# Start and end of a six-layer cross network on TensorE: row transposes, one set of weight sums, and the last addition moved

## The chip, the cores and the metric

One Trainium2 chip, one of its cores. The metric is the time of one execution on the device in microseconds: 2319.8 us, the median of 3 runs (2318.58 to 2320.22). All times below are microseconds from the start of the profiled execution unless something else is said. PE is TensorE, DVE is VectorE, ACT is ScalarE, SP is the queue of SyncE that issues most DMAs.

## The reference

```python
B, F, D, L = 16384, 100, 16, 6
Din = min(F * D, 1024)            # 1024
# x0: (16384, 1024), ws: (6, 1024, 1024), bs: (6, 1024), all bf16
x = x0
for l in range(L):
    proj = jnp.einsum('bd,de->be', x, ws[l]) + bs[l]
    x = x0 * proj + x
return x
```

Each layer multiplies the state (16384 rows of 1024) by a weight matrix, adds a bias, multiplies by the first input and adds the old state.

## The kernel before

The rows are worked through in 16 pairs of two blocks of 512 rows, and within a pair layer by layer. The state is held transposed (features on the partitions): `xst[:, n, k, :]` is feature chunk `k` of 8 for block `n`, and `x0T` holds the pair's input in the same way. A layer is a 2x2 block product: halves of the features by the two row blocks. It is done in Strassen's manner with seven half-size products, named by a number `pid`: products 1, 2 and 4 use blocks of the weight matrix as they are, products 5, 6, 3 and 7 use sums of weight blocks, and their right-hand sides are blocks of the state or the differences T1 to T4 that DVE makes (`Ops.t`). From the second pair on, product 2 is itself split into seven quarter-size products (`inner`, L287), with the differences `ti` and the *small sums*, `pid` 8, made from block W21 of the weights.

A product's matmuls go to PSUM tiles of 128x512 (`px`). There are two pools of four banks each, `ps[0]` and `ps[1]`, which change roles from layer to layer as `psA` and `psX`. ACT evicts PSUM (`ev`, L45 and L48). DVE adds the parts (L42), multiplies by `x0T` (`f_mul`) and adds the old state (`f_add`, which writes `xst`).

All weight tiles live in one ring of 12 buffers (`wring`, tile name `wp`). `prefetch_upto` issues loads on SP ten places ahead in the fixed order 1, 2, 8, 5, 3, 6, 7, 4. In the first pair the sums do not exist yet: `emit_combo(l, pid)` makes them on DVE from the raw blocks (W12 has its own tile `w`), and `flush_saves` writes each of them to a DRAM buffer `Lc`, from which all later pairs load them. DVE is busy for 24.0 us in a first-pair layer and for 20.5 us in a later one. In the first pair's layer `l` the sums 5, 6 and 3 of layer `l+1` are made after `f_add(C1, 0, 0)`, and sum 7 of layer `l+1` and the small sums of layer `l` at the end. For the last layer of the first pair, only the small sums are left, made at the end.

After each pair but the last, SP issues a DMA transpose of the finished state into the pair's own `x0T` tile (L481) and two stores of it (L484). The x0 transposes of a following pair (L474) are issued during an earlier one. The last pair's output is treated apart: its lower feature half goes through `out_region` (L231: DMA transpose, store of 512 KB), its upper half is transposed on PE by matmuls against an identity (`out_pe`, L240), evicted by ACT and DVE, and stored in pieces of 256 KB.

The start: DMA loads of x0 rows and weights are issued from SP and ACT. The first 512 rows are loaded as rows in two halves of the features (`xrows`) and transposed on PE by `transpose_rows(h)` (L204): per feature chunk four matmuls of 128x128 against the identity, then one eviction, by ACT for even chunks and by DVE for odd ones. The second 512 rows come by one DMA transpose (L193).

The order on each engine is that of the program for ACT, DVE (`pin`) and the startup DMAs. A scheduler places the other DMAs among them, and it also inserts the waits: for data, for a ring buffer or a bank that must become free, and for one of eight DMA semaphores that are used in turn.

Of the kernel before, what the change touches and what calls it, by code (L numbers as in the profile page):

```python
# [17 lines left out]
def kernel(  # L18
# [163 lines left out]
    b_all = const.tile([P, LK], FP32, name="b_all")  # L182
    x0T_next = x0t_pool.tile([P, 2, KD, NB], BF16, name="x0T")
    xrows = [ev_pool.tile([P, KH, NB], BF16, name="ev") for _ in range(2)]
    raw = {i: wring.tile([P, KH, H], BF16, name="wp") for i in (1, 2, 4)}
    combo_st[0] = {"w12": w12_pool.tile([P, KH, H], BF16, name="w12")}
    for h in range(2):
        pin(nc.sync.dma_start(xrows[h][:], x0[0:NB, h * H:(h + 1) * H].rearrange("(r p) d -> p r d", p=P)))  # L188
        if h == 0:
            pin(nc.scalar.dma_start(raw[1][:], w_src(0, 1)))  # L190
            pin(nc.sync.dma_start(b_rows[:], bs.rearrange("l (m p) -> (l m) p", p=P)))
    pin(nc.scalar.dma_start(raw[2][:], w_src(0, 2)))
    pin(nc.sync.dma_start_transpose(out=x0T_next[:, 1], in_=x0[NB:2 * NB, :]))  # L193
    pin(nc.scalar.dma_start(combo_st[0]["w12"][:], ws[0][0:H, H:D].rearrange("(k p) e -> p k e", p=P)))
    pin(nc.scalar.dma_start(raw[4][:], w_src(0, 4)))
    for i in raw:
# [4 lines left out]
    for _ in range(8):  # L201
        nc.tensor.matmul(warm[:], lhsT=zero[:, 0:P], rhs=zero[:], start=True, stop=True)

    def transpose_rows(h):  # L204
        for k in range(KH):
            pt = ps[1].tile([P, NB], FP32, name="px")
            for r in range(KH):
                nc.tensor.matmul(pt[:, r * P:(r + 1) * P], lhsT=xrows[h][:, r, k * P:(k + 1) * P], rhs=ident[:],
                                 start=(r == 0), stop=True, skip_group_check=True)
            dst = x0T_next[:, 0, h * KH + k, :]  # L210
            if k % 2 == 0:
                acopy(dst, pt[:])
            else:
                pin(nc.vector.tensor_copy(out=dst, in_=pt[:]))
# [10 lines left out]
    for pr in range(NPAIR):  # L225
# [11 lines left out]
            pin(nc.sync.dma_start(out[r0:r0 + NB, 0:H].rearrange("(j p) d -> p j d", p=P),  # L237
                                  xo_last["t"][:, n].rearrange("p j k r -> p j (k r)")))

        def out_pe(pts, n, ms, yo):  # L240
            for j in range(KH):
                for m in ms:
                    nc.tensor.matmul(pts[j][:, m * P:(m + 1) * P], lhsT=xst[:, n, KH + m, j * P:(j + 1) * P], rhs=ident[:],  # L243
                                     start=(m == 0), stop=True, skip_group_check=True)
                if ms[-1] != KH - 1:
                    continue
                if len(ms) == KH or j % 2 == 1:
                    acopy(yo[:, j, :], pts[j][:])
                else:
                    pin(nc.vector.tensor_copy(out=yo[:, j, :], in_=pts[j][:]))  # L250
                if j % 2 == 1:
                    r0 = pr * PR + n * NB + (j - 1) * P
                    pin(nc.sync.dma_start(out[r0:r0 + 2 * P, H:D].rearrange("(j p) d -> p j d", p=P), yo[:, j - 1:j + 1, :]))

        for l in range(L):
# [71 lines left out]
            if small:  # L327
                w2i = weights(8)
                wi = w2i[:].rearrange("p k (j e) -> p k j e", e=HE)
                b = cur.rhs(2)  # L330
                ti = cur.ti
                EA = ei_pool.tile([P, KH, NB], BF16, name="ea")
                EB = ei_pool.tile([P, KH, NB], BF16, name="eb")
                c11, c12 = (slice(0, 2), slice(0, NQ)), (slice(0, 2), slice(NQ, NB))
                c21, c22 = (slice(2, 4), slice(0, NQ)), (slice(2, 4), slice(NQ, NB))
                q2, q5, q1 = bank(), bank(), bank()
                for m in range(3):
                    mm(1, w1, pA, m, True)
                    ev(P1s, pA, m, 0)
                inner(q1, w2[:, 0:2, 0:HE], b[:, 0:2, 0:NQ], True)  # L340
                evi(EA[:, c11[0], c11[1]], q1)
                inner(q5, wi[:, 0], ti[:, 0], True)
                evi(EB[:, c22[0], c22[1]], q5)
                mm(1, w1, pA, 3, True)
                ev(P1s, pA, 3, 0)
                inner(q2, w2[:, 2:4, 0:HE], b[:, 2:4, 0:NQ], True)
                evi(EB[:, c11[0], c11[1]], q2)
                pX = [bank() for _ in range(KH)]
                w5 = weights(5)
                mm(5, w5, pX, 0, True)  # L350
                ev(P5s, pX, 0)
                inner(q1, wi[:, 1], ti[:, 1], False)
                evi(EA[:, c12[0], c12[1]], q1)
                inner(q5, wi[:, 2], b[:, 2:4, NQ:NB], False)
                evi(EB[:, c12[0], c12[1]], q5)
                mm(5, w5, pX, 1, True)
                ev(P5s, pX, 1)
                inner(q1, wi[:, 3], ti[:, 2], False)
                evi(EA[:, c22[0], c22[1]], q1)
                mm(5, w5, pX, 2, True)  # L360
                ev(P5s, pX, 2)
                inner(q1, w2[:, 2:4, HE:H], ti[:, 3], False)
                evi(EA[:, c21[0], c21[1]], q1)
                w3 = weights(3)
                mm(3, w3, pX, 0, False)
                ev(S53, pX, 0, 0)
                mm(5, w5, pX, 3, True)
                ev(P5s, pX, 3)
                for m in range(1, KH):
                    mm(3, w3, pX, m, False)  # L370
                    ev(S53, pX, m, 0)
                half_sum(EA, EA, EB, 0)
                cur.t(3)
                vtt(EA[:, c22[0], c22[1]], EA[:, c22[0], c22[1]], EB[:, c22[0], c22[1]], ADD)
                cur.t(4)
                vtt(C1[:, :, 0, :], P1s[:], EA[:], ADD)
            else:
                P2s = evt()
                for m in range(KH):
                    mm(1, w1, pA, m, True)  # L380
                    ev(P1s, pA, m, 0)
                    if step == 1 and m == 0:
                        transpose_rows(1)
                        ops.t(1)
                        for pid in (5, 6, 3):
                            emit_combo(0, pid)
                        ops.t(2)
                        emit_combo(0, 7)
                        flush_saves()
                pX2 = [bank() for _ in range(KH)]  # L390
                for m in range(KH):
                    mm(2, w2, pX2, m, True)
                    ev(P2s, pX2, m)
                pX = [bank() for _ in range(KH)]
                w5 = weights(5)
                for m in range(KH):
                    mm(5, w5, pX, m, True)
                    ev(P5s, pX, m)
                w3 = weights(3)
                for m in range(KH):  # L400
                    mm(3, w3, pX, m, False)
                    ev(S53, pX, m, 0)
                cur.t(3)
                cur.t(4)
                vtt(C1[:, :, 0, :], P1s[:], P2s[:], ADD)
            f_mul(C1, 0, 0)
            f_add(C1, 0, 0)
            if combos_next:
                for pid in (5, 6, 3):
                    emit_combo(l + 1, pid)  # L410
            w6 = weights(6)
            for m in range(KH):
                mm(6, w6, pA, m, False)
# [30 lines left out]
            else:  # L444
                n1, n0 = 1 ^ flip, flip
                pT = [bank() for _ in range(KH)]
                out_pe(pT, n1, range(KH), evt())
                c = lambda ms: C2[:, ms, 0, :]
                xs = lambda ms: xsrc[:, n0, KH:KD, :][:, ms, :]
                xz = lambda ms: x0T[:, n0, KH:KD, :][:, ms, :]  # L450
                parts = [slice(0, 2), slice(2, 3), slice(3, 4)]
                vtt(c(parts[0]), c(parts[0]), xz(parts[0]), MULT)
                vtt(c(parts[1]), c(parts[1]), xz(parts[1]), MULT)
                vtt(xs(parts[0]), c(parts[0]), xs(parts[0]), ADD)
                vtt(c(parts[2]), c(parts[2]), xz(parts[2]), MULT)
                vtt(xs(parts[1]), c(parts[1]), xs(parts[1]), ADD)
                vtt(xs(parts[2]), c(parts[2]), xs(parts[2]), ADD)
                pT2 = [psA.tile([P, NB], FP32, name="px") for _ in range(KH)]
                yo = evt()
                out_pe(pT2, n0, (0, 1, 2), yo)  # L460
                out_pe(pT2, n0, (3,), yo)
            if combos_next:
                emit_combo(l + 1, 7)
                emit_combo(l, 8)
                if l + 1 == L - 1:
                    stage_ctx.close()
                    xo_pool = ctx.enter_context(tc.tile_pool(name="xo", bufs=1))
            elif pr == 0:
                emit_combo(l, 8)
            if l == (2 if pr == 0 else 0) and not last_pair:  # L470
                x0T_next = x0t_pool.tile([P, 2, KD, NB], BF16, name="x0T")
                for n in range(2):
# [43 lines left out]
```

## Time and profile before

| what | us |
|---|---|
| median of 3 runs | 2319.8 |
| profiled execution, its time | 2319.24 |
| profiled execution, its span on the core | 2317.5 |
| PE busy (share of the span) | 2286.7 (99%) |
| DVE busy | 1992.9 (86%) |
| ACT busy | 1830.7 (79%) |
| mean granted TensorE clock | 0.999 |

The span is what the profile covers, from the first to the last instruction; 1.7 us of the execution lie around it. A busy PE is one that has matmuls in its pipeline; a matmul of 512 columns is shown as 0.38 long, but such matmuls start every 0.216, so the records overlap. Some records are missing, so a count in a line can be one or two short. In a timeline line the columns are the start, the length, the engine, the source line, the operation, what it writes and reads, its shape, how many such instructions in a row, and in brackets how long the engine had been idle and what ended that.

### The profile page before, as it was taken

Reading aid. Unit: us, or ns where it says so; the run is one execution under the profiler, and the core shown is the slowest. Engines: PE = TensorE matmul, PEld = TensorE weight load, DVE = VectorE, ACT = ScalarE, POOL = GpSimd, SP = SyncE. Lnnn points to the kernel's source line nnn. Section 1 sums busy time; section 2 is a strip of 40 time slices with the busy share of each in tenths; the row PEclk is TensorE's granted clock in tenths of the full one; section 3 lists DMA queues with packets and bytes.
Section 4 is the critical chain, followed back from the end, with each engine's and each line's share of the span. In section 5 each row is a group of like instructions: output and inputs, shape, how many; then the busy total and the mean of one; then the engine's idle time right before and its main releaser. Section 6 shows DMA issues by size and latency. Waiting matters only on the chain.

```text
span 2317.5 us, 31676 instructions
## 1 busy us (share of the span) xinstructions
PE 2286.7 (99%) x11675; PEld 1161.2 (50%) x11905; DVE 1992.9 (86%) x2232; ACT 1830.7 (79%) x2970; POOL 0.7 (0%) x6
## 2 busy tenths in 40 slices
PE   8999999999999999999999999999999999999998
PEld 3444554545555455555545454555545455554544
DVE  7997888888888888888888888888888888888888
ACT  6777887878788787878778787877878787887877
POOL 0000000000000000000000000000000000000000
PEclk9999999999999999999999999999999999999999
DMA  7759587595876959669586685966859578595763
GB/s 246 245 170 311 173 209 254 177 287 173 217 246 182 282 176 227 232 183 280 185 223 237 192 266 188 250 212 190 271 177 273 190 200 264 173 288 176 214 214 108
DMA packets 606618, 507.52 MB, mean 219 GB/s; under 512 B 391424, under 2 KB 545024, under 8 KB 606464
## 3 DMA queue, kind: packets, MB, share of 16 engines
q1 hardware_dynamic: 604352, 503.39, 72.6%
q10 hardware_dynamic: 2112, 2.10, 0.3%
q8 instruction: 94, 1.54, 0.3%
q14 instruction: 60, 0.49, 0.1%
HBM read 391.13 MB, written 49.28 MB: 190 GB/s over the span
## 4 chain that ended last, share of the span: by engine, by line
PE 92%; DVE 6%; issue 1%; DMA 1%; ACT 0%; SPq 0%; DVEq 0%
PE px L281 80%; PE px L287 12%; DVE cb L42 2%; DVE xst L42 1%; DVE wp L42 1%; DVE T L42 1%; DMA x0T<-in_x_dram 1%; DMA wp<-Lc 0%; ACT ev L45 0%; DVE ti L42 0%; SPq L188 0%; DVE ev L250 0%; DVEq L42 0%; DVEq L511 0%; PE px L243 0%
## 5 line engine op out<-in xcount | busy, mean ns | idle before, releaser
L281 PEld LDWEIGHTS <-wp 128*128 128x128 bf16 x9312 | 910.0, 98 | 1008.6 <-issue 5.8
L281 PE MATMUL px<-T,wp 128*128 128x512 bf16 x5992 | 1393.0, 379 | 9.1 <-DVE wp L42 1.3
L48 ACT ACTIVATE ev<-px,b_all 128x512 bf16<-128x512 f32 x1152 | 791.6, 687 | 223.1 <-PE px L281 215.1
L281 PE MATMUL px<-xst,wp 128*128 128x512 bf16 x2576 | 615.5, 379 | 5.5 <-DVE xst L42 2.0
L45 ACT CAST ev<-px 128x512 bf16<-128x512 f32 x798 | 466.7, 585 | 179.6 <-PE px L281 166.0
L42 DVE TENSOR_TENSOR cb<-cb,x0T 128x2048 bf16<-128x2048 bf16 (+1 forms) x386 | 469.9, 1218 | 9.9
L42 DVE TENSOR_TENSOR cb<-ev 128x1024 bf16<-128x1024 bf16 (+1 forms) x390 | 263.1, 696 | 231.8 <-ACT ev L45 231.8
L42 DVE TENSOR_TENSOR xst<-cb,xst 128x2048 bf16<-128x2048 bf16 x322 | 392.2, 1218 | 23.1 <-DVE cb L42 1.4
L48 ACT ACTIVATE cb<-px,b_all 128x512 bf16<-128x512 f32 x384 | 263.7, 687 | 67.8 <-PE px L281 55.2
L287 PEld LDWEIGHTS <-wp 128*128 128x128 bf16 x2520 | 246.5, 98 | 132.8 <-DMA wp<-Lc 5.3
L287 PE MATMUL px<-ti,wp 128*128 128x256 bf16 x1440 | 216.6, 273 | 4.9 <-DMA wp<-Lc 4.8
L45 ACT CAST ea<-px 128x512 bf16<-128x512 f32 x360 | 211.8, 588 | 0.0
L42 DVE TENSOR_TENSOR T<-xst,T 128x2048 bf16<-128x2048 bf16 x160 | 195.5, 1222 | 8.3
L42 DVE TENSOR_TENSOR T<-xst 128x2048 bf16<-128x2048 bf16 x160 | 194.9, 1218 | 0.0
L45 ACT CAST eb<-px 128x512 bf16<-128x512 f32 x270 | 160.2, 593 | 5.9 <-PE px L287 5.9
L287 PE MATMUL px<-xst,wp 128*128 128x256 bf16 x900 | 135.9, 274 | 0.0
L42 DVE TENSOR_TENSOR ea<-ea,eb 128x1024 bf16<-128x1024 bf16 (+1 forms) x180 | 99.9, 555 | 27.5 <-ACT eb L45 27.5
L281 PE MATMUL px<-x0T,wp 128*128 128x512 bf16 x514 | 122.7, 379 | 0.7
L42 DVE TENSOR_TENSOR cb<-ev,ea 128x2048 bf16<-128x2048 bf16 x90 | 109.7, 1218 | 0.0
L42 DVE TENSOR_TENSOR xst<-cb,x0T 128x2048 bf16<-128x2048 bf16 x64 | 78.4, 1225 | 2.2
L42 DVE TENSOR_TENSOR ti<-xst 128x512 bf16<-128x512 bf16 x150 | 63.2, 422 | 3.6
L42 DVE TENSOR_TENSOR ti<-xst,ti 128x512 bf16<-128x512 bf16 x150 | 62.7, 418 | 0.0
(29 smaller groups left out, 190.4 us busy)
## 6 DMA issues: line engine op xcount, KB each, us to landing
wp<-Lc SPq DMA_DIRECT2D x450, 512.0 KB, 3.8
wp<-in_ws_dram SPq DMA_DIRECT2D x285, 512.0 KB, 4.4
out_dram<-x0T SPq DMA_DIRECT2D x30, 1024.0 KB, 9.9
Lc<-wp SPq DMA_DIRECT2D x30, 512.0 KB, 3.4
w<-in_ws_dram SPq DMA_DIRECT2D x5, 512.0 KB, 5.9
wp<-in_ws_dram ACTq DMA_DIRECT2D x3, 512.0 KB, 8.0
ev<-in_x_dram SPq DMA_DIRECT2D x2, 512.0 KB, 6.7
out_dram<-xoS SPq DMA_DIRECT2D x2, 512.0 KB, 3.1
```

Source lines behind the costliest of these rows:

```text
L42: return pin(nc.vector.tensor_tensor(out=out, in0=in0, in1=in1, op=op))
L45: return pin(nc.scalar.copy(out=out, in_=in_))
L48: return pin(nc.scalar.activation(out=out, in_=in_, func=IDENT, bias=bias, scale=1.0))
L281: nc.tensor.matmul(pts[m][:], lhsT=wt[:, k, m * P:(m + 1) * P], rhs=rhs[:, k, :], start=(start and k == 0), stop=(k == KH - 1), **kw)
L287: nc.tensor.matmul(pt[:, m * NQ:(m + 1) * NQ], lhsT=w[:, k, m * P:(m + 1) * P], rhs=rhs[:, k, :], start=(start and m == 0 and k == 0), sto ...
```

## The change

Three things are changed. First, the second 512 rows of the first pair are loaded as rows, too (four loads in all, the last two into the tiles that later hold T3 and T4), and transposed on PE. The transposes of the four groups now stand before product 1, after product 1, and after product 2 (two groups); DVE's first weight sums stand between the last two groups and after them. Second, the last layer's small sums of the first pair are made after `f_add(C1, 0, 0)`, in the middle of that layer, and not at its end, and their save is issued there. Third, at the very end DVE no longer adds the old state for the last block's upper half: PE transposes the old state and the new part one after the other into the same PSUM banks, which adds them. The order of the two halves' transposes on PE is changed for that.

```diff
     xrows = [ev_pool.tile([P, KH, NB], BF16, name="ev") for _ in range(2)]
+    xrows += [t_pool.tile([P, KH, NB], BF16, name=f"T{i}") for i in (3, 4)]
...
-    for h in range(2):
-        pin(nc.sync.dma_start(xrows[h][:], x0[0:NB, h * H:(h + 1) * H].rearrange("(r p) d -> p r d", p=P)))
-        if h == 0:
-            pin(nc.scalar.dma_start(raw[1][:], w_src(0, 1)))
+    for q in range(4):
+        n, h = q // 2, q % 2
+        pin(nc.sync.dma_start(xrows[q][:], x0[n * NB:(n + 1) * NB, h * H:(h + 1) * H].rearrange("(r p) d -> p r d", p=P)))
+        if q == 0:
             pin(nc.sync.dma_start(b_rows[:], bs.rearrange("l (m p) -> (l m) p", p=P)))
+    pin(nc.scalar.dma_start(raw[1][:], w_src(0, 1)))
     pin(nc.scalar.dma_start(raw[2][:], w_src(0, 2)))
-    pin(nc.sync.dma_start_transpose(out=x0T_next[:, 1], in_=x0[NB:2 * NB, :]))
...
-    def transpose_rows(h):
+    def transpose_rows(q):
+        n, h = q // 2, q % 2
         for k in range(KH):
             pt = ps[1].tile([P, NB], FP32, name="px")
             for r in range(KH):
-                nc.tensor.matmul(pt[:, r * P:(r + 1) * P], lhsT=xrows[h][:, r, k * P:(k + 1) * P], rhs=ident[:],
+                nc.tensor.matmul(pt[:, r * P:(r + 1) * P], lhsT=xrows[q][:, r, k * P:(k + 1) * P], rhs=ident[:],
                                  start=(r == 0), stop=True, skip_group_check=True)
-            dst = x0T_next[:, 0, h * KH + k, :]
+            dst = x0T_next[:, n, h * KH + k, :]
...
-        def out_pe(pts, n, ms, yo):
+        def out_pe(pts, n, ms, src, start, yo):
             for j in range(KH):
                 for m in ms:
-                    nc.tensor.matmul(pts[j][:, m * P:(m + 1) * P], lhsT=xst[:, n, KH + m, j * P:(j + 1) * P], rhs=ident[:],
-                                     start=(m == 0), stop=True, skip_group_check=True)
-                if ms[-1] != KH - 1:
+                    nc.tensor.matmul(pts[j][:, m * P:(m + 1) * P], lhsT=src(m, j), rhs=ident[:],
+                                     start=(start and m == 0), stop=True, skip_group_check=True)
+                if yo is None:
                     continue
...
                     mm(1, w1, pA, m, True)
                     ev(P1s, pA, m, 0)
-                    if step == 1 and m == 0:
-                        transpose_rows(1)
-                        ops.t(1)
-                        for pid in (5, 6, 3):
-                            emit_combo(0, pid)
-                        ops.t(2)
-                        emit_combo(0, 7)
-                        flush_saves()
+                if step == 1:
+                    transpose_rows(1)
                 pX2 = [bank() for _ in range(KH)]
                 for m in range(KH):
                     mm(2, w2, pX2, m, True)
                     ev(P2s, pX2, m)
+                if step == 1:
+                    transpose_rows(2)
+                    ops.t(1)
+                    emit_combo(0, 5)
+                    emit_combo(0, 6)
+                    transpose_rows(3)
+                    emit_combo(0, 3)
+                    ops.t(2)
+                    emit_combo(0, 7)
+                    flush_saves()
...
             if combos_next:
                 for pid in (5, 6, 3):
                     emit_combo(l + 1, pid)
+            elif pr == 0:
+                emit_combo(l, 8)
+                flush_saves()
...
-                out_pe(pT, n1, range(KH), evt())
-                c = lambda ms: C2[:, ms, 0, :]
-                xs = lambda ms: xsrc[:, n0, KH:KD, :][:, ms, :]
-                xz = lambda ms: x0T[:, n0, KH:KD, :][:, ms, :]
-                parts = [slice(0, 2), slice(2, 3), slice(3, 4)]
-                vtt(c(parts[0]), c(parts[0]), xz(parts[0]), MULT)
-                vtt(c(parts[1]), c(parts[1]), xz(parts[1]), MULT)
-                vtt(xs(parts[0]), c(parts[0]), xs(parts[0]), ADD)
-                vtt(c(parts[2]), c(parts[2]), xz(parts[2]), MULT)
-                vtt(xs(parts[1]), c(parts[1]), xs(parts[1]), ADD)
-                vtt(xs(parts[2]), c(parts[2]), xs(parts[2]), ADD)
+                of_x = lambda n: (lambda m, j: xst[:, n, KH + m, j * P:(j + 1) * P])
+                of_c = lambda m, j: C2[:, m, 0, j * P:(j + 1) * P]
                 pT2 = [psA.tile([P, NB], FP32, name="px") for _ in range(KH)]
+                out_pe(pT2, n0, range(KH), of_x(n0), True, None)
+                out_pe(pT, n1, range(KH), of_x(n1), True, evt())
+                for ms in (slice(0, 2), slice(2, 3), slice(3, 4)):
+                    c = C2[:, ms, 0, :]
+                    vtt(c, c, x0T[:, n0, KH:KD, :][:, ms, :], MULT)
                 yo = evt()
-                out_pe(pT2, n0, (0, 1, 2), yo)
-                out_pe(pT2, n0, (3,), yo)
+                out_pe(pT2, n0, (0, 1, 2), of_c, False, None)
+                out_pe(pT2, n0, (3,), of_c, False, yo)
...
-            elif pr == 0:
-                emit_combo(l, 8)
```

In the prediction, group 0 to group 3 are the calls `transpose_rows(0)` to `transpose_rows(3)`.

## The prediction

> **What bounds the kernel now.** I read the share of the chain of waits first, then stretches of the timeline, then the waits of PE, DVE and SP inside the three stretches that the change touches.
>
> ```profile
> PE 92%; DVE 6%; issue 1%; DMA 1%; ACT 0%; SPq 0%; DVEq 0%
> ```
>
> PE carries the chain nearly everywhere. The 6% of DVE lie in the first pair, so that is where a change to DVE's order counts. The table of stretches (length, busy us and instructions of PE, weight loads, DVE, ACT and POOL, granted clock, DMA share, GB/s) sets one layer of the first pair against the second and third layer of the second pair, and against 3.4 us inside the former:
>
> ```profile
> 40.74:65.42 24.68, 24.30 (x110) 10.89 (x113) 24.04 (x26) 18.09 (x29) 0.00 (x0) 1.00 0.60 197
> 183.99:214.64 30.65, 25.66 (x123) 12.86 (x124) 20.45 (x24) 19.04 (x32) 0.00 (x0) 0.94 1.05 303
> 214.64:238.44 23.80, 23.69 (x124) 12.12 (x125) 20.53 (x24) 19.07 (x32) 0.00 (x0) 1.00 0.83 296
> 192.80:196.20 3.40, 3.32 (x15) 2.24 (x16) 0.00 (x0) 1.65 (x3) 0.00 (x0) 0.53 1.02 415
> ```
>
> A layer of the first pair lasts 24.68, four times over. Its 112 matmuls at 0.216 (12 in 2.75, each 0.38 long) need 24.2, so PE waits about half a microsecond per layer, for DVE: from 16.3 to 139 the list of waits has no other wait of DVE than the one at 16.37. The layer 183.99 to 214.64 is 6.85 longer than the next. PE's and DVE's timeline, then SP's:
>
> ```profile
> 6.88 1.19 PE L281 MATMUL px<-x0T,wp 128*128 128x512 bf16 x4
> 10.40 1.07 PE L208 MATMUL px<-ident,ev 128*128 128x128 bf16 x16 [2.32 <-DMA ev<-in_x_dram]
> 11.30 6.21 PE L281 MATMUL px<-x0T,wp 128*128 128x512 bf16 x27
> 18.79 1.47 PE L281 MATMUL px<-T,wp 128*128 128x512 bf16 x6 [1.28 <-DVE wp L42]
> 139.47 3.61 PE L281 MATMUL px<-xst,wp 128*128 128x512 bf16 x16 [0.28 <-DVE xst L42]
> 192.88 0.97 PE L287 MATMUL px<-ti,wp 128*128 128x256 bf16 x4 [4.84 <-DMA wp<-Lc]
> 16.37 1.23 DVE L42 TENSOR_TENSOR T<-x0T 128x2048 bf16<-128x2048 bf16 x1 [4.03 <-DMA x0T<-in_x_dram]
> 17.51 1.22 DVE L42 TENSOR_TENSOR wp<-w,wp 128x2048 bf16<-128x2048 bf16 x1
> 18.76 2.48 DVE L42 TENSOR_TENSOR wp<-wp 128x2048 bf16<-128x2048 bf16 x2
> 21.16 1.22 DVE L42 TENSOR_TENSOR T<-x0T,T 128x2048 bf16<-128x2048 bf16 x1
> ```
>
> ```profile
> 166.04 9.64 SPq L481 DMA_TRANSPOSE x0T<-xst  x1
> 175.73 0.57 SPq L108 DMA_DIRECT2D Lc<-wp  x1
> 177.56 5.93 SPq L484 DMA_DIRECT2D out_dram<-x0T  x2
> 183.58 7.32 SPq L94 DMA_DIRECT2D wp<-Lc  x5
> ```
>
> DVE's unbroken run starts at 16.37, with T1, when the DMA transpose of the second 512 rows lands. PE's last wait for it is at 139.47. Then SP: the weight tile of the small sums for pair 1, layer 1 is loaded at 183.58, behind the output transpose of pair 0 (which waits for DVE until 166.04), the save of the last small sums and two stores. It lands at 192.8; PE idles 4.84 and then works at a clock of 0.53 for 3.4 us. Idle and slow clock together are the 6.85. Last, DMA in 40 slices of the stretch 2311 to 2316.5:
>
> ```profile
> DMA  0089999999999999999999999999999999960000
> ```
>
> From 2311.4 to 2315.9 the DMA engines are full: the 512 KB store at 2310.36 and four of 256 KB leave without a gap.
>
> **The change part by part.** *Startup.* Removed: one DMA transpose. Added: two plain row loads, 32 transposes on PE, four evictions on ACT, four on DVE. PE's built order is now: group 0, sixteen matmuls of product 1, group 1, sixteen of product 2, groups 2 and 3, product 5. (a) Product 1's first four end as before; the fourth starts at 6.88+1.19-0.38 = 7.69, twelve follow until 10.50. The old gap (8.07 to 10.40, second rows landing) is filled. (b) Group 1 at 10.50 instead of 10.40. Product 2 needs its evictions at once: ACT first finishes product 1's fourth tile (ready 10.67, 0.69 long, the next 0.1 before its end), then the copy to 11.88. Product 2 runs 11.93 to 15.38. (c) Group 2 at 15.38. Its fourth bank is free after ACT's eviction of product 2's last tile (ready 15.55, done 16.17). Four transposes later, 0.43 from start to copy (10.40 to ACT's 10.83), DVE copies 16.67 to 17.35. T1 starts at 17.45 instead of 16.37: +1.09. (d) The sum of weight blocks 5 is then at 18.60 and 6 at 19.85. Now come DVE's two evictions of group 3, 0.61 apart (two such took 1.29, one 0.68), and weight sum 3 only at 19.85+1.14+1.22 = 22.21 against 20.02: +2.19. Product 5 begins at 19.87 (was 18.79), product 3 at 23.5 (was 22.25), so PE is ready for layer 2 at about 37.3, but DVE's xst is there at 36.87+2.19 = 39.1. DVE has no slack until 139.47, so all 2.19 arrive there; behind it PE has none either. Bounds: below, +1.1, where T1 keeps its time and only the evictions count; above, +3.5, where the new loads land 1.3 later than needed. I take 2.19, since every row in it is of the same shapes, 5 us away.
>
> What of the startup costs nothing: the SP queue is freed from 11.88 us of issuing the transpose, but its next loads are used by DVE from 29 on; they land earlier for no one. Groups 2 and 3 on PE lie before product 5, which DVE holds until 19.87 anyway. Eight loads of 512 KB (4.2 MB) at the 0.34 MB/us that DMA moved between 5 and 10 us are in by about 15; group 2 needs its rows at 15.38, group 3 at about 16.7, and even 19 would hide.
>
> *Small sums of the last layer.* The four DVE instructions (1.55 long together, the next one 1.46 after their start) move from 167.03 to before the half sums at 152.70 (+2.19). There DVE idles 0.72 for ACT; the rest, 0.6, is a delay of DVE until the old place. ti, needed by PE at 163.22, is there at 161.02+0.42, so 1.8 of slack cover it. No PE wait. The save and the tile's place in the weight ring move too, and SP's built order with them. The save now waits for DVE until about 156.5 and holds back the loads behind it, of which the first is used at about 180: free. The loads of small sums, 5 and 3 for pair 1, layer 1 now stand ahead of the output transpose; they wait for PE (product 7 and 4 of layer 5, product 1 of pair 1), all done by 167 in the new time. The first is used near 189. So the 4.84 and the slow clock go: -6.85. Behind the transpose (now 168.9 to 178.5) come tiles 6 and 7, used from 199 on, then the stores, two loads and the x0 transposes. That is the order which pair 2 has already (transpose at 315.64, no PE wait after it until the end), so I expect no new wait. Bounds: -6.85, or -5.0 if only the idle time goes and the clock drops elsewhere, or 0 if the load still comes late.
>
> *Tail.* DVE drops three additions (0.60, 0.35 and 0.35 on the chain), PE adds 16 transposes. The first group on PE now waits for the bank that ACT frees at 2309.77, so the other half's transposes start 0.2 late, and ACT's six copies end at 2313.5 instead of 2313.8, DVE's at 2313.2 instead of 2314.0. The last store is issued 0.5 earlier. But DMA is full until 2315.9 with bytes whose start, the store at 2310.36, does not move. I take 0; bounds -0.5 (all of it arrives) and +0.2 (the first store 0.2 late).
>
> A rule against the change stands in the Trainium skill, "TensorE: Matmul & The Clock Gate", Part 4: a PE transpose of 128x128 cost about 275 ns inside one kernel. By it the two new groups would last 4.4 each instead of 0.9, 7.0 more at the start, an estimate, and the sum would be +2.3 or 2322.1. The rows here (16 in 1.07, plain matmuls against the identity) decide.
>
> **Sum.** +2.19 - 6.85 + 0 = -4.66 on the profiled execution's 2319.24, which is 2314.6. The median of the runs is 0.56 above that execution, so 2315.1.
>
> **Rivals.** (1) *The startup is dearer*: rows land late or the new PE gaps (about 1.9 before product 5, 1.8 before layer 2) lower the clock as the gap of 4.84 did. Against: the gap of 2.32 kept 1.00. Cost +3 to +5, time 2316 to 2318. (2) *The startup is cheaper or the tail's half microsecond arrives*: 2313.4 to 2314.6. For: the last store is issued earlier; against: full DMA. (3) *The load that PE waits for only changes*: another tile behind transpose and stores comes late. For: two still stand behind it; against: the 5 to 10 us between their landing and use. Half of 6.85 back gives 2318.5. (4) *Slower*: the fourth row load lands late. It is issued only once the first weights have landed (about 6.1), and DVE's evictions of group 3 stand ahead of weight sum 3, so beyond 20.3 every microsecond counts fully. It eats the gain at a landing of 25 and costs over 0.2% at 29.6. Against: 15 by the rate.
>
> **How the numbers follow.** 0.2% of 2319.8 is 4.64, about what a measurement can tell from no change, and the forecast lies on it. Forecast (within 0.6 us) 0.58, split evenly over the line; rival 1 0.15 and rival 3 0.07, both same; rival 2 0.16, faster; rival 4 0.04, slower. Faster 0.29+0.16 = 0.45, same 0.29+0.22 = 0.51, slower 0.04. The range 2313.3 to 2318.4 goes from rival 2's end into rivals 1 and 3; outside lie the cheapest startups and rivals 3 and 4 at their worst.
>
> **What would show it.** Right: T1 near 17.4, weight sum 3 near 22.2, PE's wait before layer 2 about 1.8 (was 0.70), PE's last DVE wait of the first pair near 141.7; no wait for wp<-Lc near 190 and a layer of 23.80 there with clock 1.00; DMA full until the end and the last landing no earlier against the 512 KB store. Wrong: a gap of over 3 us with a low clock in the first 40 us, a DMA wait of PE in pair 1, or a tail shorter by 0.5.

## Result and the profile after

The changed kernel takes 2316.28 us (median of 22 runs, 2314.54 to 2317.02) against 2319.51 for the kernel before on the same chips (22 runs, 2318.58 to 2320.67). The ratio on record is 0.9984, 95% interval 0.9978 to 0.9991: about 0.16% faster (the two medians alone give 0.14%), less than the 0.2% that the prediction took as the least change that can be told from none. The forecast was 2315.1.

The median hides a structure. The 22 times fall into two groups with nothing between: nine from 2314.54 to 2315.07 (median 2314.89) and thirteen from 2316.21 to 2317.02 (median 2316.55). The profiled execution, 2314.74 with a span of 2313.0, belongs to the earlier group and is 4.5 below the profiled execution of before. The earlier group is what the forecast's sum describes; the later one, about 1.7 us above it, is what it did not see.

First the parts that went as forecast. The share of the chain of waits and three stretches of the changed kernel (columns as in the table of before: length, PE, weight loads, DVE, ACT and POOL busy, granted clock, DMA share, GB/s):

```profile
PE 92%; DVE 5%; issue 1%; DMA 0%; ACT 0%; DVEq 0%; ACTq 0%
```

```profile
42.91:67.59 24.68, 24.09 (x110) 10.87 (x113) 24.04 (x26) 18.09 (x29) 0.00 (x0) 1.00 0.58 197
186.15:209.95 23.80, 23.70 (x124) 12.12 (x124) 20.46 (x24) 19.07 (x32) 0.00 (x0) 1.00 1.03 272
209.95:233.75 23.80, 23.69 (x124) 12.14 (x125) 20.52 (x24) 19.07 (x32) 0.00 (x0) 1.00 0.87 319
```

A layer of the first pair is as long as before, 24.68, and DVE is busy for the same 24.04 of it. The second layer of the second pair, 30.65 before, is now as long as its neighbour, 23.80, at a clock of 1.00: all 6.85 are gone. SP's timeline shows why:

```profile
160.96 6.23 SPq L94 DMA_DIRECT2D wp<-Lc  x3
169.23 9.85 SPq L484 DMA_TRANSPOSE x0T<-xst  x1
180.86 6.41 SPq L487 DMA_DIRECT2D out_dram<-x0T  x2
```

Three loads of weight tiles now leave ahead of the output transpose; before, the first of them stood behind the transpose and two stores. The list of PE's waits has no load of wp<-Lc any more. The startup, PE's timeline and then DVE's:

```profile
5.73 1.07 PE L210 MATMUL px<-ident,ev 128*128 128x128 bf16 x16 [1.08 <-DMA ev<-in_x_dram]
6.91 3.78 PE L283 MATMUL px<-x0T,wp 128*128 128x512 bf16 x16
15.39 2.42 PE L210 MATMUL px<-ident,T 128*128 128x128 bf16 x32
19.87 1.69 PE L283 MATMUL px<-T,wp 128*128 128x512 bf16 x7 [2.06 <-DVE wp L42]
39.09 3.61 PE L283 MATMUL px<-xst,wp 128*128 128x512 bf16 x16 [1.64 <-DVE xst L42]
141.63 3.61 PE L283 MATMUL px<-xst,wp 128*128 128x512 bf16 x15 [0.28 <-DVE xst L42]
```

```profile
17.45 1.23 DVE L42 TENSOR_TENSOR T<-x0T 128x2048 bf16<-128x2048 bf16 x1
18.60 1.22 DVE L42 TENSOR_TENSOR wp<-w,wp 128x2048 bf16<-128x2048 bf16 x1
20.99 1.28 DVE L216 CAST x0T<-px 128x512 bf16<-128x512 f32 x2
22.19 1.22 DVE L42 TENSOR_TENSOR wp<-wp 128x2048 bf16<-128x2048 bf16 x1
```

T1 starts at 17.45, the two evictions of group 3 stand ahead of weight sum 3, which starts at 22.19 (20.02 before), and PE's last wait for DVE in the first pair is at 141.63 (139.47): a delay of 2.16 that is neither lost nor won in between. The tail, DMA in 40 slices of the stretch 2306 to 2314:

```profile
DMA  0000499999999999999999999994000000000000
```

It is full from the 512 KB store on, as it was.

Now the later group. A second profiled execution of the same kernel took 2316.31, span 2314.5. Its PE and DVE timelines:

```profile
5.68 1.89 PE L210 MATMUL px<-ident,ev 128*128 128x128 bf16 x16 [0.90 <-DMA ev<-in_x_dram]
7.65 4.73 PE L283 MATMUL px<-x0T,wp 128*128 128x512 bf16 x16
17.08 2.42 PE L210 MATMUL px<-ident,T 128*128 128x128 bf16 x32
21.56 3.74 PE L283 MATMUL px<-T,wp 128*128 128x512 bf16 x16 [2.05 <-DVE wp L42]
```

```profile
19.14 1.23 DVE L42 TENSOR_TENSOR T<-x0T 128x2048 bf16<-128x2048 bf16 x1
23.88 1.22 DVE L42 TENSOR_TENSOR wp<-wp 128x2048 bf16<-128x2048 bf16 x1
```

The first rows land at the same time (PE starts at 5.68, 0.05 earlier), but the sixteen transposes take 1.89 in place of 1.07 and product 1 takes 4.73 in place of 3.78. TensorE works at half rate until about 9.9. By group 2 it is 1.69 late, and T1 starts 1.69 later. The rest of the span is moved by nearly as much: PE's last wait for DVE in the first pair ends at 143.28 (141.63 in the earlier group's profile), and the last store lands at 2313.57 (2312.00). Weight sum 3 is again 4.74 behind T1.

### The profile page after: what moved, and what is told of

It is laid out like the page before. It is cut to its first block, busy times and chain, and to the rows that moved or that the text cites. A ratio compares the mean times of both kernels' runs of the same rounds, so it can differ in the third digit from the quotient of the medians.

```text
span 2313.0 us, 31780 instructions
## 1 busy us (share of the span) xinstructions
PE 2287.3 (99%) x11723; PEld 1163.4 (50%) x11953; DVE 1994.0 (86%) x2233; ACT 1832.8 (79%) x2974; POOL 0.7 (0%) x6
## 4 chain that ended last, share of the span: by engine, by line
PE 92%; DVE 5%; issue 1%; DMA 0%; ACT 0%; DVEq 0%; ACTq 0%
PE px L283 80%; PE px L289 12%; DVE cb L42 2%; DVE wp L42 1%; DVE xst L42 1%; DVE T L42 1%; DMA ev<-in_x_dram 0%; ACT ev L45 0%; DMA wp<-in_ws_dram 0%; DMA Lc<-wp 0%; DVE x0T L216 0%; PE px L210 0%; DVE ti L42 0%; ACT cb L48 0%; ACT ev L48 0%
```

## Experiments

Theory A is the forecast's sum: the three parts add up, startup +2.2, small sums -6.85, tail 0. The two groups of times were not in it, and for them there were three places to look (startup, middle, tail) before the profile above was seen.

**Startup alone.** The edit is the startup's part of the change on the kernel before:

```diff
+    xrows += [t_pool.tile([P, KH, NB], BF16, name=f"T{i}") for i in (3, 4)]
...
-    pin(nc.sync.dma_start_transpose(out=x0T_next[:, 1], in_=x0[NB:2 * NB, :]))
...
+                if step == 1:
+                    transpose_rows(2)
...
+                    transpose_rows(3)
```

> The kernel before with the startup of the change alone. Theory A (the terms simply add): +2.2 on 2319.5, so 2321.7; T1 on DVE near 17.45, weight sum 3 near 22.2, PE's last wait for DVE of the first pair near 141.7, and in pair 1 the wait for wp<-Lc (4.84) and the layer of 30.65 as before. Rival (the later DVE is taken up by slack of the first pair): under +1, below 2320.5. On the two groups of times that the changed kernel shows, about 1.5 us apart (2314.5 to 2315.1 and 2316.2 to 2317.0): theory S says that they come from the startup, where PE's transposes now hang on the landing of six loads; then they appear here too, about 2321.3 and 2322.8, and a profile from the later group has the 1.5 us before 40 us. Theories M (middle) and T (tail): one group here.

Measured: 2322.36 against 2319.33, ratio 1.0013 (1.0004 to 1.0023). Of the eleven runs one took 6697.77. Of the other ten, five lie from 2321.52 to 2321.91, four from 2323.02 to 2324.0, and one between at 2322.36. The lower five are 2.2 to 2.6 above before: theory A's +2.2. The ten times hint at the two groups, here where neither the small sums nor the tail are changed, but they do not show them: the kernel before spreads over as much. In the profile weight sum 3 is at 22.43, PE's last wait for DVE at 141.84, and PE still waits 4.46 for wp<-Lc. It also shows something of rival 1 of the forecast. PE's timeline and a stretch of it:

```profile
20.11 5.31 PE L283 MATMUL px<-T,wp 128*128 128x512 bf16 x16 [2.06 <-DVE wp L42]
39.33 3.61 PE L283 MATMUL px<-xst,wp 128*128 128x512 bf16 x16
```

```profile
19.80:24.00 4.20, 3.89 (x12) 1.51 (x13) 4.17 (x6) 1.17 (x2) 0.00 (x0) 0.67 0.84 317
```

In this execution the new gap of 2.06 did lower the clock (0.67; product 5 takes 5.31, not 3.74). It cost nothing: layer 2 starts 21.64 after T1 here (39.33 less 17.69) and 21.64 after T1 in the changed kernel (39.09 less 17.45), because DVE sets that start and PE merely has no wait left. The margin is small: the matmuls before it end at 39.23.

**Small sums alone.**

```diff
             if combos_next:
                 for pid in (5, 6, 3):
                     emit_combo(l + 1, pid)
+            elif pr == 0:
+                emit_combo(l, 8)
+                flush_saves()
...
-            elif pr == 0:
-                emit_combo(l, 8)
```

> The kernel before with the last layer's small weight sums of the first pair made before product 6 alone. Theory A: -6.85, so 2312.7, with no wait of PE for wp<-Lc and 23.80 for the second layer of pair 1; this would beat both kernels. Rival (the startup's later DVE helped the load order or the gain is partly that of another part): -4.7 or less, 2314.8 or more. Two groups of times: theory M (new SP order in pair 1) has them here, 2312.2 and 2313.7; theories S and T one group.

Measured: 2312.33 (2312.05 to 2312.60), ratio 0.997 (0.9958 to 0.9981), 7.0 below before: theory A, the whole gain from this part. One group, so the middle is cleared of the two groups. Its profiled execution, PE and then DVE, says more:

```profile
5.53 1.89 PE L208 MATMUL px<-ident,ev 128*128 128x128 bf16 x16 [0.75 <-DMA ev<-in_x_dram]
10.35 1.89 PE L208 MATMUL px<-ident,ev 128*128 128x128 bf16 x16 [0.96 <-DMA ev<-in_x_dram]
```

```profile
16.16 1.23 DVE L42 TENSOR_TENSOR T<-x0T 128x2048 bf16<-128x2048 bf16 x1 [3.19 <-DMA x0T<-in_x_dram]
```

TensorE is at half rate here too, even longer than in the later group above, and the execution takes 2312.28, no more than the others. In the old startup T1 waits for a DMA transpose, whatever PE does, and PE's lateness is used up by PE's own waits: product 5 starts at 18.74 without a wait (at 18.79 after one of 1.28 before the change), and layer 2 still waits 0.54 for DVE (0.70).

**Tail alone.**

```diff
-                vtt(xs(parts[0]), c(parts[0]), xs(parts[0]), ADD)
...
+                out_pe(pT2, n0, range(KH), of_x(n0), True, None)
...
+                out_pe(pT2, n0, (0, 1, 2), of_c, False, None)
```

> The kernel before with the last block's old state added on TensorE alone. Theory A: 0, so 2319.5 within 0.3, DMA full from the 512 KB store to the last landing. Rival (the last store's half microsecond arrives): 2319.0. Two groups of times: theory T (the stores contend differently from run to run) has them here, 1.5 us apart; theories S and M one group.

Measured: 2319.82 against 2319.33, ratio 1.0002 (0.9993 to 1.0011). That agrees with 0, but the interval reaches from -1.6 to +2.6, so the times alone do not rule out -0.5. The spread, 2319.13 to 2320.66, is no wider than that of the kernel before and shows no two groups. The profiles tell more. SP's timeline in the tail, of the kernel before and then of this one:

```profile
2310.36 0.38 SPq L237 DMA_DIRECT2D out_dram<-xoS  x1
2311.39 3.00 SPq L253 DMA_DIRECT2D out_dram<-ev  x4
```

```profile
2310.27 0.38 SPq L237 DMA_DIRECT2D out_dram<-xoS  x1
2311.48 2.43 SPq L253 DMA_DIRECT2D out_dram<-ev  x4
```

The 512 KB store leaves 0.09 earlier than before in these executions. The issue of the last store ends 0.48 earlier (2313.91, before 2314.39), and its landing is only about 0.03 earlier (2316.40, before 2316.43). From the end of PE's last product to the last landing it is 7.43 here and 7.38 before; in three profiles with the changed tail and the changed startup it is 7.48 to 7.64.

**The changed kernel again.** No edit; its profile is the second one shown above.

> The changed kernel once more on the same chip as its three parts. Theory A: the three differences to the kernel before add up to this one's within 0.5 us, -4.66 in the earlier group of times. Two groups of times again; a profile from the later group shows where its 1.5 us lie: before 40 us (theory S), between 150 and 240 us (M), or after 2300 us (T).

Measured: 2316.31, five runs from 2314.74 to 2315.23, six from 2316.31 to 2316.59. The earlier group is 4.3 below before's 2319.33; the three parts (+2.3 for the lower five of the startup, -7.0, and the tail) sum to -4.7 with the tail at 0 and to -4.2 with its +0.5 taken at face value. The profile puts the later group's time before 20 us: the startup.

**The rate of TensorE, by the matmuls of zeros ahead.** The kernel has eight of them, from 1.19 to about 4.8; the first rows land at about 5.7.

```diff
-    for _ in range(8):
+    for _ in range(4):
```

> The changed kernel with 4 matmuls of zeros ahead of the first transposes in place of 8. Theory C (the two groups of times are TensorE at half rate or full rate from 5.7 us on; the changed kernel's T1 on DVE hangs on TensorE's first 90 instructions, so 1.65 us of slow TensorE arrive at the end): TensorE stops at 2.9 and is at half rate at 5.7 in every run, with 16 transposes in 1.89 in place of 1.07; no run in the earlier group (2314.5 to 2315.1), all at 2316.2 to 2318.5, T1 at 19.1 or later. Rival D (the loads land later in some executions, and the rate of TensorE does not matter): the same two groups as before.

```diff
-    for _ in range(8):
+    for _ in range(10):
```

> The changed kernel with 10 matmuls of zeros ahead of the first transposes in place of 8, so that TensorE has almost no gap (0.1 in place of 0.9 to 1.1) before them. Theory C: the slow stretch, which went on to about 9.9 in the slow execution seen, ends by about 8; the later group comes nearer by a half or more: runs between 2314.5 and 2316.0, median about 2315.2. Rival D: the same two groups, 2314.5 to 2315.1 and 2316.2 to 2317.0.

Measured with 4: 2316.71, 2315.82 to 2317.32, no run in the earlier group (three lie up to 0.4 below the 2316.2 that was expected as the least). With 10: 2314.77, 2314.46 to 2314.97, no run in the later one (11 runs each). PE's timeline with 4, then with 10:

```profile
5.78 1.89 PE L210 MATMUL px<-ident,ev 128*128 128x128 bf16 x16 [2.70 <-DMA ev<-in_x_dram]
7.75 5.35 PE L283 MATMUL px<-x0T,wp 128*128 128x512 bf16 x16
```

```profile
5.76 1.07 PE L210 MATMUL px<-ident,ev 128*128 128x128 bf16 x16 [0.93 <-DMA ev<-in_x_dram]
6.95 3.63 PE L283 MATMUL px<-x0T,wp 128*128 128x512 bf16 x16
19.75 2.02 PE L283 MATMUL px<-T,wp 128*128 128x512 bf16 x7 [2.06 <-DVE wp L42]
22.00 3.07 PE L283 MATMUL px<-T,wp 128*128 128x512 bf16 x8 [0.22 <-issue]
24.90 3.62 PE L283 MATMUL px<-x0T,wp 128*128 128x512 bf16 x16
```

The rows land at the same time in both, so rival D (late loads) falls, and the rate is set by what PE did before. Two instructions without any result to compute move the whole kernel's median by 1.5. That all runs with 10 are early went beyond theory C, which had a remnant up to 2316.0; why there is none is not shown. It is not the shorter gap that was expected (0.1): PE idled 0.93 here, too. In this execution the gap before product 5 halved the rate as in the startup alone (5.15 from product 5 to product 3; 3.59 in the changed kernel), and at 2314.46 it is still the fastest of the eleven.

**The same on the old startup.** The kernel with the small sums alone, with `range(4)` in place of `range(8)`.

```diff
-    for _ in range(8):
+    for _ in range(4):
```

> The kernel with the small sums moved and the startup of before, with 4 matmuls of zeros ahead of the first transposes in place of 8. Theory C (the startup of before hangs on the DMA transpose that lands at 16.24, not on TensorE): TensorE is at half rate at 5.7 in every run and the time stays where it was with 8, 2312.0 to 2312.6. Rival (a slow TensorE at the start costs any startup its 1.5 to 2 us, and the runs with 8 happened to be alike): 2313.8 or more.

Measured: 2312.35 (2312.08 to 2312.59) against 2312.33 with 8. Half rate until about 13.7 in its profile, and no cost: the sensitivity belongs to the new startup.

**Evictions of group 3 on ACT.**

```diff
-            if k % 2 == 0:
+            if q == 3 or k % 2 == 0:
                 acopy(dst, pt[:])
```

> The changed kernel with all four evictions of the fourth transposed group on ACT. Theory A (the two evictions on DVE that stand ahead of weight sum 3 cost 1.1, and DVE has no slack up to 140 us): weight sum 3 at 21.0 after T1 at 17.45 and the whole kernel 1.1 faster, groups 2313.4 to 2314.0 and 2314.9 to 2315.9. Rival (DVE is late by T1 only, or ACT's four copies delay product 5's evictions): 0 to -0.4.

Measured: 2313.96; six runs from 2313.69 to 2313.96, five from 2315.36 to 2315.93: the groups' medians are 1.1 and 0.9 below those of the changed kernel. DVE's timeline of its profiled execution, one of the later group:

```profile
19.33 1.23 DVE L42 TENSOR_TENSOR T<-x0T 128x2048 bf16<-128x2048 bf16 x1
20.47 1.22 DVE L42 TENSOR_TENSOR wp<-w,wp 128x2048 bf16<-128x2048 bf16 x1
21.72 2.48 DVE L42 TENSOR_TENSOR wp<-wp 128x2048 bf16<-128x2048 bf16 x2
```

Sums 6 and 3 follow each other without the evictions between. So of the startup's 2.2, about 1.1 were the evictions ahead of sum 3 and 1.1 the later T1, as the forecast had it.

**T1 early.** The third row load takes the place of weight block 12 in its queue; group 2 is transposed before product 2, T1 and sums 5 and 6 right behind; group 3's evictions go to ACT.

```diff
+    rows(nc.sync, 1)
+    pin(nc.sync.dma_start(combo_st[0]["w12"][:], ws[0][0:H, H:D].rearrange("(k p) e -> p k e", p=P)))
+    rows(nc.sync, 3)
...
+    rows(nc.scalar, 2)
...
                 if step == 1:
                     transpose_rows(1)
+                    transpose_rows(2)
+                    ops.t(1)
+                    emit_combo(0, 5)
+                    emit_combo(0, 6)
```

> The changed kernel with the third row load ahead of the weight block 12, the third group transposed before product 2, T1 and weight sums 5 and 6 right behind, and the fourth group's evictions on ACT. Theory A (the end of the first pair follows DVE's start, 16.37 before and 17.45 in the changed kernel): T1 near 14.0, weight sum 3 near 17.6 in place of 22.2 (20.0 before); up to 4.6 faster than the changed kernel if DVE alone counts, 2310.2 to 2311.5 in the earlier group; the last DVE wait of the first pair near 137 to 138. Rival (with DVE early TensorE becomes the bound, which starts product 5 only near 17.6 and has 0.5 of slack a layer): 2312 to 2313, and PE's DVE waits of the first pair gone.

Measured: 2312.24 in five runs, one at 2311.05 and four from 2312.21 to 2312.91. The profiled one (2312.64) is at half rate at the start, with T1 at 15.77. With the rate settled:

```diff
-    for _ in range(8):
+    for _ in range(10):
```

> The early rows with 10 matmuls of zeros ahead in place of 8. Theory C: the five times of early rows, 2311.05 and 2312.2 to 2312.9, are again the full and the half rate of TensorE at the start (its profile, at 2312.64, has 16 transposes in 1.89); with 10 all runs are near 2311.0, within 0.4. It would be the fastest so far, 1.3 below the small sums alone. Rival (TensorE carries this startup by its instruction count, so the rate of the first 3 us is not what spreads the times): 2311 to 2313 again.

Measured: 2310.86 (2310.68 to 2310.94), ratio to before 0.9961 (0.9949 to 0.9974): 1.5 below the small sums alone, 3.9 below the changed kernel with 10 matmuls ahead, and the fastest here. PE's timeline (L214 are transposes, L287 products) and DVE's:

```profile
10.23 1.06 PE L214 MATMUL px<-ident,ev 128*128 128x128 bf16 x16
11.92 1.07 PE L214 MATMUL px<-ident,T 128*128 128x128 bf16 x16 [0.63 <-DMA T<-in_x_dram]
17.76 3.61 PE L287 MATMUL px<-T,wp 128*128 128x512 bf16 x16
137.52 3.61 PE L287 MATMUL px<-xst,wp 128*128 128x512 bf16 x16 [0.28 <-DVE xst L42]
```

```profile
13.97 1.23 DVE L42 TENSOR_TENSOR T<-x0T 128x2048 bf16<-128x2048 bf16 x1
16.37 2.48 DVE L42 TENSOR_TENSOR wp<-wp 128x2048 bf16<-128x2048 bf16 x2
19.21 1.22 DVE L42 TENSOR_TENSOR T<-x0T,T 128x2048 bf16<-128x2048 bf16 x1 [0.36 <-ACT x0T L45]
```

T1 is at 13.97 and PE's last wait for DVE at 137.52, 4.1 earlier than in the changed kernel. The wait is still there, so the rival (TensorE as the bound) did not come true by the end of the pair; DVE's lead of about 4.5 at weight sum 3 arrived but for half a microsecond. That half is lost at once: DVE then waits 0.36 for an eviction by ACT, and T2 at 19.21 is 4.11 earlier than in the changed kernel (23.32).

**Is the tail bound by bytes?** On the changed kernel with 10 matmuls ahead; the first two of the last four stores are left out, so the right half of one block of 512 rows is not written.

```diff
-                if j % 2 == 1:
+                if j % 2 == 1 and not start:
                     r0 = pr * PR + n * NB + (j - 1) * P
```

> The changed kernel with 10 matmuls of zeros ahead (2314.46 to 2314.97), and of the last four stores the first two left out, so the last two columns' half of one block of 512 rows is not written: 512 KB less at the end. Theory A (the end is set by bytes: five landings 0.77 apart from 2308.86 to 2311.72, so an earlier last store gains nothing): the last landing comes forward to where the last store's own path lets it, 2.0 after its issue at 2309.2, so 0.5 less, 2314.3. Rival (the end is the last store's own path from ACT's last copy, and the three additions taken off DVE did not shorten it): 0, 2314.8.

Measured: 2314.05 (2313.87 to 2314.34) against 2314.77: 0.7 less (0.5 expected). In its profile the last store lands 2.08 after the end of its issue (2309.38 to 2311.46); with all stores it took 2.54 (2309.18 to 2311.72). DMA in 40 slices of 2306 to 2314, with all stores and then without the two:

```profile
DMA  0008999999999999999999999800000000000000
```

```profile
DMA  0000008999999600099999996000000000000000
```

Now there is a hole between the 512 KB store and the last two, and the end is that of these two stores' own path. With all stores the hole is filled, and an earlier last store waits behind the others' bytes. From the end of PE's last product to the last landing it is 6.96 here, and 7.48 with all stores.

## Why the prediction was right and where not

- *Startup, (a) to (c), T1 +1.09.* Right for a TensorE at full rate: 17.45 by forecast and by profile. Wrong as a statement on the kernel: "product 1's first four end as before" took the rate of one execution of before for a property of the program. At half rate T1 is at 19.14. This is the step that failed, together with the last one of the sum, "the median of the runs is 0.56 above that execution": that offset was measured on a startup that a DMA transpose shields from PE. The missing term is 1.7 in 13 of 22 runs, which is enough to carry the median from 2314.9 to 2316.3. With it the startup costs about 3.9, more than the +3.5 that was its upper bound. It was not among the rivals. Rival 1 had its price and its resource, the clock, but put it in the gaps that the change makes; those were free in the two profiles in which one of them slowed TensorE.
- *Startup, (d), +2.19.* Right: sum 3 at 22.19 (forecast 22.21), the shift at the last DVE wait 2.16. Taking the evictions off DVE returned about the 1.1 that they were priced at, and starting T1 early returned nearly all of its lead. DVE has no slack in the first pair.
- *Costs set to nothing in the startup.* Right: the row loads land by 15.4 (forecast 15), group 3 lies in PE's wait before product 5, which was 2.06 (forecast 1.9), and the wait before layer 2 was 1.64 (forecast 1.8).
- *Small sums, -6.85.* Right in the profile (30.65 to 23.80), -7.0 alone. No new wait, so rival 3 falls.
- *Tail, 0.* Right in the mechanism and nearly in size: 0.48 earlier at the last store's issue is about 0.03 at its landing; take bytes away and the end moves. In the changed kernel's profile the 512 KB store leaves 0.28 late against PE (4.41 earlier than before, where PE's last product ends 4.69 earlier), a little over the 0.2 that was the upper bound. The DMA transpose ahead of that store landed 4.58 after its issue there, 4.25 before; in the tail alone it took 4.26, so the change of the tail does not explain it.
- *Rival 4 (late fourth load).* Did not occur: it landed at 15.3.
- *Sum.* -4.66 against -4.69 at the end of PE's last product, -4.5 between the profiled executions, and -4.62 between the earlier group's median and that of before. The median of all runs moved by -3.2, and 2316.28 is 1.2 from the forecast, twice the 0.6 that it gave itself.
- *Luck.* The median lies in the stated range only because the range ran up to 2318.4 for rivals 1 and 3. Neither happened: the later group comes from a cause that the range was not made for.
- *A reading.* "The 6% of DVE lie in the first pair" holds for about three quarters: DVE has 61% of the chain up to 160 us, some 98 us, and the rest lies in later pairs and the tail.

## What to carry to other kernels

Before moving work from a DMA to an engine, ask what each of them inherits from the time before: the DMA transpose cut DVE's chain off from TensorE's start-up rate (2312.33 and 2312.35 with 8 and 4 matmuls ahead), and the transposes on TensorE tied a chain without slack to it. Look at the single run times, not only at the median: two groups with nothing between them call for a cause, and a profile of one execution of each shows where to look. A combined change can hide a good part behind a bad one: here one third of the edit is worth 7.0 us and another costs 2.2 or 3.9.

## What the runs showed of the hardware

- TensorE starts at half rate in all 13 profiles and goes over to full rate at a moment that differs from execution to execution of the same program. At half rate matmuls of 512 columns start about 0.43 apart (eight of zeros take 3.60 and four 1.89), at full rate 0.216 (16 take 3.61, 12 take 2.75). With eight matmuls of zeros the moment lay near 4.4 in one execution of the changed kernel and near 9.9 in the other; with four, near 11.3. With the old startup, in which PE has gaps, it lay before 5.7 in the kernel before, near 9 in the tail alone, and near 13.3 and 13.7 in the two kernels with the small sums moved. The Trainium skill, "TensorE: Matmul & The Clock Gate", Part 1, says that an activity window of about 3.4 us that runs freely, not reset by the kernel's start, decides this, and that the same kernel therefore shows different counts of slow matmuls. The traces agree with the variation. They do not explain why 10 matmuls, which ended by 5.1 in the profiles seen (eight by 4.8), left no slow run in 25 (three kernels).
- The granted clock of the profile does not show this rate. A stretch of the second execution of the changed kernel, in which 16 transposes took 1.89, reads 1.00:

```profile
5.70:9.90 4.20, 4.20 (x23) 2.58 (x24) 1.49 (x3) 1.49 (x3) 0.00 (x0) 1.00 1.01 348
```

- Gaps of PE of the same length act differently: the 2.06 before product 5 left the rate alone in both executions of the changed kernel and halved it in the one of the startup alone and in the one with 10 matmuls ahead. After such a gap the granted clock does show it (0.67 in the startup alone). What decides it is not shown.
- The kernels that keep the wait of 4.5 to 4.8 in the second pair spread over 1.5 us and more (before 2.1, tail alone 1.5); without that wait, and with the rate at the start settled or shielded, the spread is 0.3 to 0.6 (small sums 0.55, ten matmuls 0.51, early rows with ten 0.26). That the clock after the wait makes the spread is likely (0.53 over 3.4 us in one execution, 0.60 over 3.6 in another) but not shown.
